# Attention, two MLPs: the fourth unit's attention by float16 halves and DMA transposes instead of transposes on TensorE

## The chip, the cores and the metric

The kernel runs on one core of one Trainium2 chip. The metric is the device time of one execution in microseconds (us). Before the change it is 997.64 us, the median of 3 runs (997.09 to 998.67).

## The reference

Causal attention with a decay (batch 4, 8 heads, 576 positions, head size 64) is followed by two MLPs on the 2304 x 512 result, with 2048 inner features each.

```python
scores = scale * np.matmul(q, k.transpose(0, 1, 3, 2))
cum = np.cumsum(np.log(np.clip(f, 0.0001, 1.0)), axis=-1)
scores = np.where(causal, -1e9, scores + cum[:, :, :, None] - cum[:, :, None, :])
attn = np.exp(scores - np.max(scores, axis=-1, keepdims=True))
attn = attn / (np.sum(attn, axis=-1, keepdims=True) + 1e-09)
x = (attn @ v) laid out as (B*S, H*D)
x = (s * np.maximum(x @ w_in, 0.0) ** 2 + b) @ w_out        # first MLP
h = x @ w_in2
out = np.maximum(0.01 * h, h) @ w_out2                       # second MLP
```

## The kernel before

**Units.** The attention and the first MLP are cut into units. Units 0 to 3 are the first 256 positions of the four batches, units 4 to 7 the last 320 positions, whose queries see up to 576 keys; unit 8 collects the last 64 positions of the four batches for the MLP. Units 0 and 1 go through the first MLP together (the loop with `u == 1`, 16 steps, `joint_step`), while the attention of unit 2 is computed beside it. Then each unit from 2 on has 16 steps of `first_mlp`, and the attention of the unit behind it is spread over those steps. The steps are counted by `n` = 16(u - 2) + i. Unit 3, the fourth, has its attention in steps 0 to 8, beside the MLP of unit 2; units 4 to 7 have theirs from step 10 on.

**One step.** `first_mlp` issues 12 matmuls into `ps_h` (`mlp1_h`, L941), then Relu, Square and a copy to float32r on ScalarE (L970 to L972) and a subtraction on VectorE (L974) that leaves the low half of g; then the 12 matmuls of an earlier step from g into `ps_o` (`mlp1_back`, `mlp1_o`, L991). From step 2 on the g used is that of two steps before. The bank of `ps_h` alternates between two, so the matmuls of step n wait until L974 of step n - 2 has read its bank. Below, H is the first group of 12, O the second.

**The attention of a pair of heads.** The heads go in pairs; p = 8 to 11 are the pairs of unit 3, 12 to 27 those of units 4 to 7. The dictionary `plan`, filled ahead by `at_step`, says what each step does; `attend`, `attend_early`, `attend_mid` and `attend_end` do it. In all units the scores are formed on TensorE (`mm_score`, L297, with the mask, L307; below, S) in one PSUM buffer `ps_s`, the maxima are taken by VectorE (`score_max`, L335), which asks SyncE for later `cumk` and `qk_p` loads (L231, L205) as it goes, and ScalarE takes the exponentials (`score_exp`, L357).

- Unit 3 (pair p scored in step 2(p - 8)): in the same step VectorE builds diagonal matrices of the reciprocal sums (`diags`, `pair_diag`, L377 to L381). In the next step TensorE multiplies the exponentials with them, which transposes and scales them (`turn_pair`, `turn`, L779), and ScalarE copies the result (L398). In the step after that TensorE multiplies with v in float32 (`pair_av`, `first_av`, L787), and `first_x` splits the result (L801, L802). v comes as it is wanted, in two loads for the whole unit (`load_v_in(3)`, L579), issued in step 14 of the joint loop.
- Units 4 to 7 (a pair in four steps): p is scaled and cut in float16 halves (`p_scale`, L403, L404; `p_high`, L421, on ScalarE; `p_low`, L426, on VectorE), and each head's halves are transposed by a DMA from SyncE (L434). The second head's `p_high`, `p_low` and transpose are issued in the next step (`carry`). Three steps after the scores `av_mm` multiplies (L484); `av_copy` (L510, ScalarE), `av_add` (L514, VectorE) and `av_end` with `split_x1` (L546, L547) finish. v takes the same road, once a pair: `load_v` (L217) into one buffer `v_raw` that all pairs share; `v_part(p, 0)`, which is `scale_v` (a maximum over v_raw, L244, three small operations, L248 to L252, on VectorE, and the high half on GpSimd, L257); `v_part(p, 1)`, which is `halve_v` (L263 on VectorE, two DMA transposes, L268) and right behind it `load_v(p + 1)`.

In units 4 to 7 the load of v for a pair is issued three steps ahead of the `v_part(.., 0)` that reads it.

**What sets the order.** All of this stands under `in_order()`: each engine, SyncE with its DMA queue included, does its instructions in exactly the order in which the code issues them. An instruction that waits holds back all behind it on its engine.

Of the kernel before, what the change touches and what calls it, by code (L numbers as in the profile page):

```python
# [8 lines left out]
F32 = mybir.dt.float32  # L9
# [8 lines left out]
P = 128  # L18
# [31 lines left out]
def attention_moe_moe_kernel(  # L50
# [748 lines left out]
    def first_x(u, pr, raw):  # L799
        x = xs[u]  # L800
        nc.scalar.copy(x[:, 0, pr], raw)  # L801
        nc.vector.tensor_tensor(out=x[:, 1, pr], in0=raw, in1=x[:, 0, pr].bitcast(F32), op=ALU.subtract)  # L802
# [14 lines left out]
    plan = {}  # L817

    def at_step(n):
        return plan.setdefault(n, {k: [] for k in ("v", "early", "s", "av", "x", "turn", "diag", "first", "load")})  # L820

    t_of = {}
    for i, (jb, *_) in enumerate(tiles):
# [1 line left out]
    nxt = 0  # L825
    for p in range(H, NP):
        ids = t_of[p]
        at_step(nxt)["s"] = ids[:2]
        if len(ids) == 2:
            at_step(nxt)["diag"] = at_step(nxt + 1)["turn"] = at_step(nxt + 2)["first"] = ids  # L830
            nxt += 2
            if len(t_of[p + 1]) > 2:
                at_step(nxt)["load"].append(p + 1)
                at_step(nxt + 1)["v"].append((p + 1, 0))
                nxt += 2
                at_step(nxt)["early"].append((p + 1, 1))
        else:
            for k in range(3):
                at_step(nxt + k)["s"] = ids[2 * k : 2 * k + 2]
                at_step(nxt + 3 + k)["av"] += ids[2 * k : 2 * k + 2]  # L840
            at_step(nxt + 6)["x"].append(ids[-1])
            if p + 1 < NP:
                at_step(nxt + 3)["early"].append((p + 1, 0))
                at_step(nxt + 4)["early"].append((p + 1, 1))
            nxt += 4
    assert max(plan) < 5 * NF

    def attend(n):
        e = at_step(n)
        first = e["s"] and len(t_of[jobs[tiles[e["s"][0]][0]][2] // 2]) == 2  # L850
        tail = e["s"] and jobs[tiles[e["s"][0]][0]][3]
        if ended:
            mlp1_end(*ended.pop())
        if e["first"]:
            k = e["first"][-1]
            first_x(3, jobs[tiles[k][0]][1] // 2, pair_av(3, k))
        if e["s"] and not tail:
            mm_score(e["s"][0])
        for i in carry:
            p_high(i)  # L860
            p_low(i)
        carry.clear()
        if tail:
            return
        for i in e["s"]:
            score_max(i)
        for i in e["s"]:
            score_exp(i)
        for p, part in e["early"]:
            v_part(p, part)  # L870
        if not first:
            for i in e["s"]:
                p_scale(i)
            for i in e["s"][:1]:
                p_high(i)
                p_low(i)
            carry.extend(e["s"][1:])

    def attend_early(n):
        diags(at_step(n)["diag"])  # L880
        for i in at_step(n)["s"]:
            if jobs[tiles[i][0]][3]:
                st_score(i)

    def attend_mid(n):
        e = at_step(n)
        turn_pair(e["turn"])
        for part in (av_mm, av_copy, av_add):
            for i in e["av"]:
                part(i)  # L890
        for i in e["s"]:
            if jobs[tiles[i][0]][3]:
                p_scale(i)
                p_high(i)
                p_low(i)
# [13 lines left out]
            load_v(p + 1)  # L909

    def attend_end(n):
        e = at_step(n)
        for p in e["load"]:
            load_v(p)
        for p, part in e["v"]:
            v_part(p, part)
        for i in e["x"]:
            av_end(i)

    hn = [0]  # L920
# [78 lines left out]
    def mlp1_end(u, po):  # L999
# [14 lines left out]
        for d in (2, 1, 0, 3) if u < 2 else range(ND):  # L1014
            x1 = x1d[d * P : (d + 1) * P, :]
            if u < 2:
                o = p_tile(F32) if d in (0, 3) else ap.tile([P, S], F32, tag="tt", name="x1o", bufs=4)[:, : 2 * UN]
                if d % 2 == 0:
                    nc.scalar.mul(o, po[d], sb[:, 0:1])
                else:  # L1020
                    nc.vector.tensor_scalar(o, po[d], sb[:, 0:1], None, ALU.mult)
                last = nc.sync.dma_start(
                    out=x1.rearrange("p (b s) -> p b s", b=B)[:, :2, :UN], in_=o.rearrange("p (b s) -> p b s", b=2)
                )
                continue
# [127 lines left out]
    def joint_step(i):  # L1153
# [19 lines left out]
        turn_pair(t)  # L1173
        if pending:
            mlp1_back(1)
        if i == NF - 2:
            load_v_in(3)
        pending.append((1, i, g))
        high(w1, c_of, i)

# [9 lines left out]
    for u in range(1, NU):  # L1190
# [12 lines left out]
        for i in range(NF):  # L1203
# [10 lines left out]
            if u < NU - 2:  # L1214
                n = (u - 2) * NF + i
                with in_order():
                    if n == 0:
                        rest.pop()()
                        for k in range(ND):
                            first_x(2, k, x_held[k])  # L1220
                    attend(n)
                    if n == 1:
                        attend_mid(n)
                        first_mlp(u, i)
                    else:
                        first_mlp(u, i, lambda: attend_early(n), lambda: attend_mid(n))
                    attend_end(n)
                continue
            with in_order():
# [98 lines left out]
```

## Time and profile before

| | |
|---|---|
| median of 3 runs | 997.64 us (997.09 to 998.67) |
| the profiled execution | 999.24 us |
| its span, first to last instruction | 997.4 us |
| PE busy | 976.8 us (98%) |
| DVE busy | 524.5 us (53%) |
| ACT busy | 506.8 us (51%) |
| GpSimd (POOL) busy | 28.3 us (3%) |

PE is TensorE's matmuls, PEld its weight loads, DVE VectorE, ACT ScalarE, SPq the DMAs that SyncE issues. "Idle before" and "<-" name how long an engine was idle ahead of an instruction and what ended that. The shares are means over the span; the stretch that the change touches lies between 130 and 192 us. A float32 matmul shows as two instructions.

### The profile page before, as it was taken

The numbers are of one execution on the slowest core, as the hardware profiler recorded it, in microseconds if no ns is written. First come the engines' busy times: TensorE is split into PE (matmuls) and PEld (weight loads), VectorE is DVE, ScalarE is ACT, GpSimd is POOL, SyncE is SP. The second block draws the span as 40 slices with busy tenths as digits, with TensorE's granted clock in tenths as the row PEclk, the third lists the DMA queues.
The fourth block names the chain that finished last, engine by engine and source line by source line (L and its number), as shares of the span: only waits on it lengthen the run. The fifth ranks groups of instructions, "written<-read, shape, count | busy, mean of one in ns | idle before, by whom it ended". The sixth has DMA issues, their size and how long they took to land.

```text
span 997.4 us, 17061 instructions
## 1 busy us (share of the span) xinstructions
PE 976.8 (98%) x6464; PEld 833.2 (84%) x6464; DVE 524.5 (53%) x1307; ACT 506.8 (51%) x1196; POOL 28.3 (3%) x100
## 2 busy tenths in 40 slices
PE   6899999999999999999999999999999999999998
PEld 5677779898888888888999998888888888888897
DVE  7797864477777777777312689783113111211121
ACT  6777766576776767767544665552122221212222
POOL 1000000000000000000000000000000000000000
PEclk9999999999999999999999999999999999999999
DMA  9744314299999998897200992003000100100010
GB/s 327 244 148 149 85 64 119 70 202 194 180 184 189 192 186 184 183 189 153 54 22 1 332 373 97 1 1 127 1 1 22 43 0 1 43 1 1 1 43 22
DMA packets 157105, 110.31 MB, mean 111 GB/s; under 512 B 110624, under 2 KB 135200, under 8 KB 157024
## 3 DMA queue, kind: packets, MB, share of 16 engines
q1 hardware_dynamic: 157024, 109.23, 43.3%
q8 instruction: 51, 0.84, 0.3%
q14 instruction: 30, 0.25, 0.1%
HBM read 74.00 MB, written 10.04 MB: 84 GB/s over the span
## 4 chain that ended last, share of the span: by engine, by line
PE 52%; ACT 0%; DVE 0%; issue 0%
PE ps_o L1091 20%; PE ps_h L1075 20%; PE ps_o L991 6%; PE ps_h L941 6%; PE ps_v L484 0%; DVE o L1103 0%; ACT tt L357 0%; ACT p_hl L421 0%; DVE g L974 0%; ACT g L972 0%; ACT ps_h L971 0%; ACT ps_h L970 0%
## 5 line engine op out<-in xcount | busy, mean ns | idle before, releaser
L941 PE MATMUL ps_h<-x_all,w 128*128 128x256 f32 (+1 forms) x1536 | 230.3, 299 | 1.7 <-ACT r_all L956 0.7
L991 PE MATMUL ps_o<-g,w 128*128 128x256 f32 (+2 forms) x1536 | 231.2, 300 | 0.0
L1091 PE MATMUL ps_o<-w,g 128*128 128x512 f32 x864 | 215.0, 395 | 0.0
L941 PEld LDWEIGHTS ps_h<-x_all,w 128*128 128x128 f32 x1536 | 202.1, 189 | 13.9 <-DVE g L974 3.9
L1075 PE MATMUL ps_h<-x,w 128*128 128x512 f32 (+1 forms) x960 | 213.5, 370 | 0.0
L991 PEld LDWEIGHTS ps_o<-g,w 128*128 128x128 f32 x1536 | 203.1, 189 | 10.7
L1075 PEld LDWEIGHTS ps_h<-x,w 128*128 128x128 f32 x960 | 169.1, 188 | 34.4
L1091 PEld LDWEIGHTS ps_o<-w,g 128*128 128x128 f32 x864 | 161.0, 188 | 37.5
L1083 DVE TENSOR_TENSOR g<-ps_h,g 128x512 fp32r<-128x512 f32 (+1 forms) x80 | 50.9, 637 | 248.8 <-ACT g L1082 248.5
L1081 ACT ACTIVATE ps_h<-ps_h 128x512 f32<-128x512 f32 (+1 forms) x80 | 43.1, 539 | 263.2 <-PE ps_h L1075 263.2
L357 ACT ACTIVATE tt<-tt,sm 128x256 f32<-128x256 f32 (+3 forms) x112 | 68.9, 616 | 76.2 <-DVE sm L335 76.2
L974 DVE TENSOR_TENSOR g<-ps_h,g 128x256 fp32r<-128x256 f32 x112 | 47.2, 421 | 86.7 <-ACT g L972 86.7
L970 ACT ACTIVATE ps_h<-ps_h 128x256 f32<-128x256 f32 x112 | 40.9, 365 | 51.9 <-PE ps_h L941 51.9
L335 DVE CUSTOM_DVE_ANT_0 tt<-ps_s,cumk 128x256 f32<-128x256 f32 (+3 forms) x112 | 54.1, 520 | 2.1 <-PE ps_s L307 0.7
L426 DVE SCALAR_TENSOR_TENSOR p_hl<-tt,sm,p_hl 128x512 f16<-128x512 f32 (+1 forms) x64 | 44.8, 700 | 15.6 <-ACT p_hl L421 14.4
L1082 ACT CAST g<-ps_h 128x512 fp32r<-128x512 f32 (+1 forms) x80 | 43.6, 544 | 6.5 <-PE ps_o L1091 4.1
L124 DVE SCALAR_TENSOR_TENSOR wt<-w_raw,wt 128x512 int32<-128x512 int32 x64 | 44.4, 694 | 2.2
L421 ACT ACTIVATE p_hl<-tt,sm 128x512 f16<-128x512 f32 (+1 forms) x64 | 42.6, 665 | 4.3 <-ACT tt L357 3.0
L972 ACT CAST g<-ps_h 128x256 fp32r<-128x256 f32 x112 | 41.8, 373 | 4.3
L971 ACT ACTIVATE ps_h<-ps_h 128x256 f32<-128x256 f32 x112 | 41.2, 368 | 3.6
L484 PE MATMUL ps_v<-p_t,v_st 128*128 128x128 f16 (+1 forms) x768 | 42.7, 209 | 0.0
L119 ACT ACTIVATE wt<-w_raw 128x512 f32<-128x512 f32 x64 | 41.0, 674 | 0.8 <-DMA w_raw<-in_moe_w_out 0.6
(123 smaller groups left out, 780.7 us busy)
## 6 DMA issues: line engine op xcount, KB each, us to landing
w_raw<-in_moe_w_in SPq DMA_DIRECT2D x32, 512.0 KB, 7.9
w_raw<-in_moe_w_out SPq DMA_DIRECT2D x32, 512.0 KB, 9.1
cumk<-cumd SPq DMA_DIRECT2D x32, 256.0 KB, 4.1
qk_p<-in_qk SPq DMA_DIRECT2D x16, 480.0 KB, 4.5
cumk<-cumd SPq DMA_DIRECT2D x32, 144.0 KB, 3.4
v_raw<-in_v SPq DMA_DIRECT2D x16, 288.0 KB, 3.3
out<-o SPq DMA_DIRECT2D x18, 256.0 KB, 2.1
x2r<-x1d SPq DMA_DIRECT2D x4, 1024.0 KB, 5.9
```

The source lines that it names most:

```text
L124: nc.vector.scalar_tensor_tensor(x, top, -0x80000000, x, ALU.bitwise_and, ALU.bitwise_or)
L335: nc.vector.tensor_tensor_reduce(tt[:, at + k0 : at + k0 + kw], ps[:, c, :kw] if half else ps[:, h % 2, at : at + w], cumk[jb][:, k0 : k0 ...
L357: nc.scalar.activation(e, e, AF.Exp, bias=sm[:, r : r + 1], scale=-1.0, accum_out=sm[:, 2 + r : 3 + r])
L426: nc.vector.scalar_tensor_tensor(v[:, 1, :w], e, inv, v[:, 0, :w], ALU.mult, ALU.subtract)
L941: nc.tensor.matmul(ps, wi[:, a, d * P : (d + 1) * P], x_all[:, :, c, d] if joint[0] else x[:, c, d], start=(d == 0 and n == 0), stop=(d == ...
L974: nc.vector.tensor_tensor(out=g[:, 1, :UN], in0=ps, in1=g[:, 0, :UN].bitcast(F32), op=ALU.subtract)
L991: nc.tensor.matmul(po[d], wo[:, a, d * P : (d + 1) * P], g[:, c], start=(first and n == 0), stop=(last and n == 2),)
L1075: nc.tensor.matmul(ps[:, :n], wi[:, a, d * P : (d + 1) * P], x[:, e, d, :n], start=(d == 0 and k == 0), stop=(d == ND - 1 and k == 2),)
L1081: nc.scalar.activation(raw, raw, AF.Lrelu)
L1082: nc.scalar.copy(g[:, 0, :n], raw)
L1083: nc.vector.tensor_tensor(out=g[:, 1, :n], in0=raw, in1=g[:, 0, :n].bitcast(F32), op=ALU.subtract)
L1091: nc.tensor.matmul(po[m], g[:, a, m * P : (m + 1) * P], wo[:, e, :], start=(i == 0 and k == 0), stop=(i == NF - 1 and k == 2),)
```

## The change

Unit 3's attention is computed as that of units 4 to 7, in a plan of two steps a pair.

- Pair p (8 to 11) is scored in step 2(p - 8) as before. `p_scale`, `p_high`, `p_low` and the first head's DMA transpose follow in that step, the second head's in the next; `av_mm` with copy and add comes three steps after the scores, `av_end` four steps after. The diagonals, the turn on PE, the copies of its result, the float32 product and `first_x` of unit 3 are gone.
- `v_part(p + 1, 0)` is issued in the odd step behind pair p's scores, `v_part(p + 1, 1)` in the next even step. The first pair's v is loaded in step 13 of the joint loop, scaled in step 15, and `v_part(8, 1)` is issued in step 0. For pair 12 `v_part` moves from steps 9 and 10 to steps 7 and 8.
- The joint MLP's end writes two of its four outputs through the buffers `p_t0` and `p_hl_t` instead of `p_hl`.
- The separate order of step 1, where the turn stood ahead of the step's matmuls, is gone.

```diff
         ids = t_of[p]
-        at_step(nxt)["s"] = ids[:2]
         if len(ids) == 2:
-            at_step(nxt)["diag"] = at_step(nxt + 1)["turn"] = at_step(nxt + 2)["first"] = ids
-            nxt += 2
-            if len(t_of[p + 1]) > 2:
-                at_step(nxt)["load"].append(p + 1)
-                at_step(nxt + 1)["v"].append((p + 1, 0))
-                nxt += 2
-                at_step(nxt)["early"].append((p + 1, 1))
+            at_step(nxt)["s"] = at_step(nxt + 3)["av"] = ids
+            at_step(nxt + 4)["x"].append(ids[-1])
+            at_step(nxt + 1)["early"].append((p + 1, 0))
+            at_step(nxt + 2)["early"].append((p + 1, 1))
+            nxt += 2 if len(t_of[p + 1]) == 2 else 4
...
     def attend(n):
         e = at_step(n)
-        first = e["s"] and len(t_of[jobs[tiles[e["s"][0]][0]][2] // 2]) == 2
...
-        if e["first"]:
-            k = e["first"][-1]
-            first_x(3, jobs[tiles[k][0]][1] // 2, pair_av(3, k))
...
         for p, part in e["early"]:
             v_part(p, part)
-        if not first:
-            for i in e["s"]:
-                p_scale(i)
-            for i in e["s"][:1]:
-                p_high(i)
-                p_low(i)
-            carry.extend(e["s"][1:])
+        for i in e["s"]:
+            p_scale(i)
+        for i in e["s"][:1]:
+            p_high(i)
+            p_low(i)
+        carry.extend(e["s"][1:])

     def attend_early(n):
-        diags(at_step(n)["diag"])
...
     def attend_mid(n):
         e = at_step(n)
-        turn_pair(e["turn"])
...
             if u < 2:
-                o = p_tile(F32) if d in (0, 3) else ap.tile([P, S], F32, tag="tt", name="x1o", bufs=4)[:, : 2 * UN]
+                if d in (0, 3):
+                    o = ap.tile([P, 5 * P], F32, tag=("p_t0", "p_hl_t")[d % 2], name="x1o", bufs=1)[:, : 2 * UN]
+                else:
+                    o = ap.tile([P, S], F32, tag="tt", name="x1o", bufs=4)[:, : 2 * UN]
...
-        if i == NF - 2:
-            load_v_in(3)
+        if i == NF - 3:
+            load_v(H)
+        if i == NF - 1:
+            v_part(H, 0)
...
                     if n == 0:
+                        at_step(n)["early"].append((H, 1))
                         rest.pop()()
...
                     attend(n)
-                    if n == 1:
-                        attend_mid(n)
-                        first_mlp(u, i)
-                    else:
-                        first_mlp(u, i, lambda: attend_early(n), lambda: attend_mid(n))
+                    first_mlp(u, i, lambda: attend_early(n), lambda: attend_mid(n))
                     attend_end(n)
```

## Rows read from the trace of the kernel before

**Rows 1.** The page, part 1: busy time, share of span, instructions.

```profile
PE 976.8 (98%) x6464; PEld 833.2 (84%) x6464; DVE 524.5 (53%) x1307; ACT 506.8 (51%) x1196; POOL 28.3 (3%) x100
```

**Rows 2.** Windows, from S of step 4 to S of step 6: us, busy by engine, clock, DMA share, GB/s.

```profile
167.93:177.01 9.08, 9.08 (x82) 8.46 (x80) 3.48 (x14) 5.22 (x17) 0.00 (x0) 1.00 0.39 100
```

**Rows 3.** Timeline, PE from H of step 5: start, length, what, idle before.

```profile
171.93 1.59 PE L941 MATMUL ps_h<-x_all,w 128*128 128x256 f32 x12
...
173.35 1.50 PE L779 MATMUL ps_t<-diag,tt 128*128 128x128 f32 x12
...
174.61 1.67 PE L991 MATMUL ps_o<-g,w 128*128 128x256 f32 x12
...
176.21 0.87 PE L787 MATMUL av<-p_t,v_in 128*64 128x256 f32 x8
...
177.01 0.92 PE L297 MATMUL ps_s<-qk_p 64*128 64x256 f32 x8
```

**Rows 4.** Timeline, PE in a step of unit 4's attention.

```profile
210.38 0.84 PE L484 MATMUL ps_v<-p_t,v_st 128*128 128x128 f16 x12
211.03 1.67 PE L991 MATMUL ps_o<-g,w 128*128 128x256 f32 x12
212.63 0.92 PE L297 MATMUL ps_s<-qk_p 64*128 64x384 f32 x4
```

**Rows 5.** Timeline: step 0 around the maxima, a load of step 6, S of step 10.

```profile
149.84 0.92 PE L297 MATMUL ps_s<-qk_p 64*128 64x256 f32 x8
...
151.13 0.42 DVE L335 CUSTOM_DVE_ANT_0 tt<-ps_s,cumk 128x256 f32<-128x256 f32 x1
...
152.24 0.08 DVE L335 DVE_READ_ACCUMULATOR2_ANT sm<- 128x1 f32 x1
...
152.78 0.38 SPq L205 DMA_DIRECT2D qk_p<-in_qk  x1
...
180.80 0.54 SPq L205 DMA_DIRECT2D qk_p<-in_qk  x1
...
191.92 1.13 PE L297 MATMUL ps_s<-qk_p 64*128 64x512 f32 x4
```

**Rows 6.** SyncE's DMA queue: v's transposes, the load behind them; all transposes of p (min/median/max ns).

```profile
195.57 2.65 SPq L268 DMA_TRANSPOSE v_st<-v_hl  x2
198.33 0.53 SPq L217 DMA_DIRECT2D v_raw<-in_v  x1
...
L434 SPq DMA_TRANSPOSE p_t<-p_hl x64: 1209/1237/2207, 199.0 to 475.4; - x64
```

**Rows 7.** From issue to landing: line L217, 288 KB; loads of 128 KB, steps 0 to 7.

```profile
DMA to landing us min/median/max: 3.1/3.3/4.1
...
cumk<-cumd SPq DMA_DIRECT2D x5, 128.0 KB, 3.4
```

**Rows 8.** Groups by form, DVE: busy us, mean ns, idle before.

```profile
L718 DVE TENSOR_REDUCE sm<-ps_s 128x1 f32<-128x256 f32 x4 | 1.7, 416 | 0.0
...
L252 DVE RECIPROCAL vs<-vs 128x1 f32<-128x1 f32 x16 | 2.6, 164 | 0.6
...
L974 DVE TENSOR_TENSOR g<-ps_h,g 128x256 fp32r<-128x256 f32 x72 | 30.2, 420 | 24.9 <-ACT g L972 24.9
...
L514 DVE TENSOR_TENSOR x_raw<-ps_v,x_raw 64x256 f32<-64x256 f32 x30 | 12.7, 422 | 5.4 <-ACT x_raw L510 5.2
...
L244 DVE TENSOR_REDUCE vs<-v_raw 128x1 f32<-128x576 f32 x16 | 11.9, 745 | 0.0
...
L426 DVE SCALAR_TENSOR_TENSOR p_hl<-tt,sm,p_hl 128x384 f16<-128x384 f32 x31 | 20.0, 647 | 5.6 <-ACT p_hl L421 5.5
```

**Rows 9.** Opening: PE behind a wait (timeline), and its clock after (windows, PE alone).

```profile
34.99 1.18 PE L679 MATMUL ps_s<-qk_p 64*128 64x128 f32 x8 [1.73 <-DMA qk_p<-in_qk]
...
36.00:37.00 1.00, 1.00 (x8) 0.50 0.60 149
...
39.00:40.00 1.00, 1.00 (x10) 1.00 0.74 157
```

More of the change, by code (lines that the diff above doesn't have):

```diff
@@ L819, in at_step @@
     def at_step(n):
-        return plan.setdefault(n, {k: [] for k in ("v", "early", "s", "av", "x", "turn", "diag", "first", "load")})
+        return plan.setdefault(n, {k: [] for k in ("early", "s", "av", "x")})
     t_of = {}
@@ L911, in attend_end @@
     def attend_end(n):
[L912 to L917, printed above, removed]
+        for i in at_step(n)["x"]:
             av_end(i)
```

## The prediction, made before the changed kernel ran

> **What bounds the kernel now.** I read the page's busy times first: TensorE (PE) is busy for 976.8 of 997.4 us, VectorE (DVE) and ScalarE (ACT) for about half [rows 1]. As the shares are means over stages, I then read the stretch that the change touches, unit 3's attention in steps 0 to 9. From one S to the next but one, two steps later, PE is busy for all of 9.08 us, DVE for 3.48, ACT for 5.22, at a granted clock of 1.00 [rows 2]. No wait of PE is listed there: PE's instructions in a row set the pace, and the other engines have 4 to 5 us of slack per pair of heads. From the first score of step 0 at 149.84 to that of step 10 at 191.92 it takes 42.08 us [rows 5]. Behind step 10 the order of the work is nearly as before, so the change is worth what it does to these 42.08 us.
>
> **Off PE.** Start to start, the turn takes 173.35 to 174.61 = 1.26 us and the float32 product 176.21 to 177.01 = 0.80 us a pair [rows 3]. The float16 product of 12 matmuls of 128 columns that takes their place lasts 0.65 us (210.38 to 211.03) [rows 4]: it has the same count here, as unit 3's heads have two and one blocks of keys in two halves, for two heads. Net 1.41 us a pair, 5.6 us for four. The sums on PE alone say 5.6 us faster.
>
> **Onto DVE.** Gone a pair are the diagonals and one subtraction of the split; added are four small operations of `p_scale` (0.16 each [rows 8]), four `p_low`, `scale_v`, `halve_v`, two `av_add` (0.42 each) and a split. `p_low` on 256 and on 128 columns is not in the trace; the row of 384 columns, 0.65, bounds it from above, and the 256-wide subtraction L974, 0.42, is about its lower end, so I take 0.53 and 0.41 (an estimate), and 0.5 each for `halve_v` and the split. With starts some 0.03 us apart: maxima 1.2 [rows 5], halve 0.5, scale 0.75, four p_low 1.9, two L974 0.9, `scale_v` 1.05, adds 0.86, split 0.5, together 7.65 us a pair. PE would need 9.08 - 1.41 = 7.67. So DVE goes from 3.5 of 9.1 us to the whole of PE's new pace, and in its fixed order it also waits some 0.8 us a pair for exponentials. The slack that hid its waits is gone.
>
> **Onto SyncE, and the wait that matters.** The change adds four DMA transposes and one load of v a pair. `halve_v` of pair p issues two transposes of v and behind them `load_v(p + 1)`; the very next step issues `scale_v(p + 1)`, whose first operation on DVE reads that load. In units 4 to 7 three steps lie between; here one. What is queued on DVE behind this wait: L974 of the odd step (which frees the bank for H two steps on), `av_add`, and the next pair's maxima, which lead to the next `halve_v`, the next transposes and the next load. So it is a loop that goes round once a pair, and I sum it. Let M be the start of a pair's maxima (151.13 in step 0).
> - SyncE first issues two `cumk` loads and one `qk` load, which is out at 153.16, so M + 2.03 [rows 5]. The maxima take to 152.32, M + 1.2, and `halve_v` is done by M + 1.75, under that.
> - Two transposes of v, then the load: from 195.57 to 198.33, 2.76 us [rows 6]. The load goes out at M + 4.8. The transposes here are smaller than the 640 columns of that row. The 64 transposes of p there have 768 or 1024 columns and still all lie near 1.24 us (1.21 at the least) [rows 6], so I take the price as fixed. The ends: 1.21 each, and, if they were as cheap as a plain load, 0.44 each (the `qk` loads took 0.38 and 0.54 [rows 5]).
> - Landing: 3.1 to 4.1 us for v at 288 KB, 3.4 for loads of 128 KB [rows 7], which is the size here; I take 3.3. It lands at M + 8.1.
> - `scale_v`: a maximum over 256 columns 0.42 and three operations of 0.16 [rows 8], with gaps 1.05; L974, 0.45. Done at M + 9.55.
> - two `av_add`, 0.86 [rows 8], then the next M: M + 10.4. Into step 2 there is no `av_add` yet: M + 9.55.
>
> Each round thus takes 10.4 us where PE needs 7.7 and took 9.08 before. M is 151.13, then 160.7, 171.1 and 181.5 in step 6. In the last round SyncE is 1.0 later, as step 6 loads more for the larger unit (the `qk` load ends at 181.34, 4.33 behind S [rows 3, 5], against 3.32 in step 0): the load of pair 12 goes out at M + 5.8, lands at M + 9.1 (288 KB); `scale_v` over 576 columns takes 0.75 + 0.6, L974 0.45: M + 10.95 = 192.45. H of step 9 waits for that. Behind it stand H 1.42 (171.93 to 173.35), the float16 product 0.65 and O 1.60 (211.03 to 212.63) [rows 3, 4]: the score of step 10 starts at 196.1 instead of 191.92. **4.2 us later.**
>
> **PE's clock.** By this sum PE idles about 1.0 us ahead of H of step 5, 2.0 ahead of step 7 and 3.5 ahead of step 9. In the opening PE came back at 34.99 after a wait of 1.73, and its granted clock was then 0.50, which is 1.2 GHz, in 36 to 37 and back at 1.00, 2.4 GHz, by 39 [rows 9]; it had been busy before, with gaps. Such a dip of about 2.8 us costs 1.4 us where PE is on the path, and here it is only behind step 9. I take half, 0.7 (ends 0 and 1.4). The earlier gaps would dip into idle time.
>
> **At no cost.** v's first load and scaling lie in steps 13 and 15 of the joint loop, where DVE waits for ACT; if not, a microsecond. The outputs of the joint end go out through other buffers, with the same work. ACT has some 6.8 us of work in 10.4, SyncE about 7 (four transposes of 1.3, four loads of 0.45).
>
> **A page beside the row.** The transpose of v takes SyncE 1.3 us each, a plain load 0.38 to 0.54 [rows 5, 6]. The Trainium skill, "Advanced Engine Details and Errata", section "X-Bar Transpose (TRN2)", says that on this chip transposing DMAs are as fast as regular ones. By the row the loop is 10.4 us a round; by that rule it would be rival 2 below.
>
> **The sum.** 4.2 + 0.7 = 4.9 us. The profiled execution took 999.24 us (span 997.4 and 1.84 around it), so 1004.1 there; it lies 1.60 above the median, so I predict **1002.5 us**.
>
> **The rivals.**
> 1. PE's sum holds whole: 997.6 - 5.6 = 992.0. For it: PE is the bound everywhere else, and H has two banks, so the first late round costs PE nothing (H of step 3 comes as late as the loop's 160.7). Against it: DVE's 7.65 leaves nothing for waits, and the lateness of each round adds up. 7%.
> 2. The load lands in time or goes out early, as with transposes of 0.44: out at M + 3.0, landed at M + 6.3, round 8.7; DVE's own work and waits, 8.4 to 8.5, are then the floor. M in step 6 is 151.13 + 8.5 + 17.4 = 177.0, L974 of step 7 done at 186.2, the score of step 10 at 189.85: 2.1 us faster, and up to 3.9 with no wait for the load at all. Time about 994.8, and this is the one on the other side, faster; it decides where a round is under some 9.3 us, that is if load and transposes together are 1.1 us quicker than summed. For it: the small v transposes are not in the trace. Against it: the even price over sizes. 14%.
> 3. Slower still: landing at 4.1 each time, as transposes of p and v share the queue, adds 0.8 a round, 3.2 in all, and a full dip of the clock 0.7 more: 1006.4. For it: in units 4 to 7 the slowest landing is 4.1. Against it: the DMA share here is 0.39 [rows 2]. 9%.
>
> **How the numbers follow.** The forecast has 70%; its own range goes from +2.6 (landing 3.1, transposes at 1.21, no dip) to +7 (landing 3.9, full dip): 1000.2 to 1004.9. For 8 in 10 the range must take in most of rival 2 and the near half of rival 3: 994.5 to 1006. About 0.2%, 2 us, is what a measurement of this kernel can tell from no change. Slower by more than that (over 999.6): nearly all of the forecast, 0.64, and rival 3, together 0.73. Within: 0.06 of the forecast and 0.04 of rival 2, 0.10. Faster: rival 1 and the rest of rival 2, 0.17.
>
> **What would show it.** Right: in the changed trace the maximum over v_raw (L244) stands idle for a DMA, about 1 us or more, in steps 1, 3, 5 and 7; the starts of the maxima lie 9.5 to 10.5 us apart; PE waits ahead of H (L941) in steps 5, 7 and 9, released by DVE's L974; two transposes of v take 2.5 us of SyncE's queue. Wrong: L244 starts without a wait, maxima 7.7 to 8.7 apart; or PE without idle time between steps 0 and 10. If DVE idles for exponentials more than for the load, the bound is DVE's and ACT's chain, and the loop only its neighbour.

## The result, and the profile after

The kernel after takes 1004.74 us, the median of 4 runs (1004.08 to 1005.98); the kernel before took 998.15 us in 4 runs beside it. The ratio is 1.0064, with a 95% interval of 1.0048 to 1.0081: slower by about 6.5 us. The profiled execution took 1005.98 us (span 1004.2), against 999.24 us (span 997.4) before. The executions of one kernel spread over 1 to 6 us, and step 0 begins between 148.6 and 152.5 us in the profiles. So each kernel below is also judged by the length from the first score of step 0 to that of step 10 in its profile. Such a length stands for one execution: experiments 4 and 11 are the same kernel and differ in it by 0.9 us. Line numbers have moved: H is now L926, O L976, the subtraction on VectorE (DVE) behind H L959.

The page's part 1 of the kernel after (busy us, share of the span, instructions; it answers to [rows 1]):

```profile
PE 975.6 (97%) x6432; PEld 832.8 (83%) x6432; DVE 537.1 (53%) x1355; ACT 511.3 (51%) x1212; POOL 31.1 (3%) x108
```

TensorE (PE) is busy 1.2 us less, DVE 12.6 more, and the execution is 6.7 us longer. A share over 1000 us can't show where. The waits of PE and DVE from 145 to 205 us can (engine, line waited for: us in total, times, longest). In the kernel before PE has none in this stretch. The kernel after has these:

```profile
DVE vs L244 <- DMA v_raw<-in_v: 12.1, 4, 4.3
...
PE ps_h L926 <- DVE g L959: 6.5, 3, 3.2
...
PE ps_v L484 <- DMA p_t<-p_hl: 1.4, 1, 1.4
...
PE ps_h L926 <- ACT x1o L1007: 0.5, 1, 0.5
```

DVE stands 12.1 us for the load of v, in four places, and PE 6.5 us for DVE's subtraction, 6.3 of them in the two waits behind the late loads. Two short waits of PE are new besides: for the transposed p, once, and for a copy of the joint MLP's output out of `ps_o`, once.

The timeline of the kernel after, PE and DVE (start, length, what, idle before), at the scores, the first maxima of each pair, the maxima over v_raw and two late H:

```profile
149.79 0.92 PE L297 MATMUL ps_s<-qk_p 64*128 64x256 f32 x8
...
151.08 0.43 DVE L335 CUSTOM_DVE_ANT_0 tt<-ps_s,cumk 128x256 f32<-128x256 f32 x1
...
158.19 0.42 DVE L244 TENSOR_REDUCE vs<-v_raw 128x1 f32<-128x256 f32 x1 [0.58 <-DMA v_raw<-in_v]
...
159.42 0.42 DVE L335 CUSTOM_DVE_ANT_0 tt<-ps_s,cumk 128x256 f32<-128x256 f32 x1
...
169.02 0.42 DVE L244 TENSOR_REDUCE vs<-v_raw 128x1 f32<-128x256 f32 x1 [4.33 <-DMA v_raw<-in_v]
...
171.13 0.42 DVE L335 CUSTOM_DVE_ANT_0 tt<-ps_s,cumk 128x256 f32<-128x256 f32 x1
...
180.60 0.42 DVE L244 TENSOR_REDUCE vs<-v_raw 128x1 f32<-128x256 f32 x1 [3.78 <-DMA v_raw<-in_v]
...
181.97 1.76 PE L926 MATMUL ps_h<-x_all,w 128*128 128x256 f32 x12 [3.15 <-DVE g L959]
...
182.71 0.42 DVE L335 CUSTOM_DVE_ANT_0 tt<-ps_s,cumk 128x256 f32<-128x256 f32 x1
...
191.83 0.75 DVE L244 TENSOR_REDUCE vs<-v_raw 128x1 f32<-128x576 f32 x1 [3.44 <-DMA v_raw<-in_v]
...
193.54 2.81 PE L926 MATMUL ps_h<-x_all,w 128*128 128x256 f32 x12 [3.15 <-DVE g L959]
...
198.85 1.13 PE L297 MATMUL ps_s<-qk_p 64*128 64x512 f32 x4
```

From step 0 to step 10 it is now 198.85 - 149.79 = 49.06 us, where it was 42.08 [rows 5]: 6.98 longer, which is about the whole result. The maxima start at 151.08, 159.42, 171.13 and 182.71: rounds of 8.34, 11.71 and 11.58 us. Each pair waits for its load of v, and the last two H shown for the DVE work behind that.

### The profile page after: what moved, and what is told of

Same layout as the page of the kernel before. It is cut to its first block, busy times and chain, and to the rows that moved or that the text cites. A ratio compares the mean times of both kernels' runs of the same rounds, so it can differ in the third digit from the quotient of the medians.

```text
span 1004.2 us, 17130 instructions
## 1 busy us (share of the span) xinstructions
PE 975.6 (97%) x6432; PEld 832.8 (83%) x6432; DVE 537.1 (53%) x1355; ACT 511.3 (51%) x1212; POOL 31.1 (3%) x108
## 4 chain that ended last, share of the span: by engine, by line
PE 52%; ACT 0%; DVE 0%; issue 0%
PE ps_o L1079 20%; PE ps_h L1063 20%; PE ps_o L976 6%; PE ps_h L926 6%; PE ps_v L484 0%; DVE o L1091 0%; ACT tt L357 0%; ACT p_hl L421 0%; DVE g L959 0%; ACT g L957 0%; ACT ps_h L956 0%; ACT ps_h L955 0%
## 5 line engine op out<-in xcount | busy, mean ns | idle before, releaser
L926 PE MATMUL ps_h<-x_all,w 128*128 128x256 f32 (+1 forms) x1536 | 231.8, 300 | 8.6 <-DVE g L959 6.5
L976 PE MATMUL ps_o<-g,w 128*128 128x256 f32 (+2 forms) x1536 | 232.4, 301 | 0.0
L926 PEld LDWEIGHTS ps_h<-x_all,w 128*128 128x128 f32 x1536 | 203.2, 190 | 21.7 <-DVE g L959 10.7
L976 PEld LDWEIGHTS ps_o<-g,w 128*128 128x128 f32 x1536 | 204.2, 190 | 10.7
L959 DVE TENSOR_TENSOR g<-ps_h,g 128x256 fp32r<-128x256 f32 x112 | 47.1, 421 | 78.2 <-ACT g L957 78.1
L426 DVE SCALAR_TENSOR_TENSOR p_hl<-tt,sm,p_hl 128x512 f16<-128x512 f32 (+2 forms) x80 | 50.9, 645 | 15.2 <-ACT p_hl L421 13.6
L421 ACT ACTIVATE p_hl<-tt,sm 128x512 f16<-128x512 f32 (+2 forms) x80 | 48.9, 621 | 4.0 <-ACT tt L357 3.3
L484 PE MATMUL ps_v<-p_t,v_st 128*128 128x128 f16 (+1 forms) x816 | 47.4, 212 | 1.4 <-DMA p_t<-p_hl 1.4
L484 PEld LDWEIGHTS <-v_st 128*128 128x128 f16 x816 | 39.1, 99 | 3.9 <-issue 1.5
```

The costliest lines, as they stand in the source:

```text
L421: nc.scalar.mul(v[:, 0, :w], e, inv)
L426: nc.vector.scalar_tensor_tensor(v[:, 1, :w], e, inv, v[:, 0, :w], ALU.mult, ALU.subtract)
L484: nc.tensor.matmul(av[:, at + e * m : at + (e + 1) * m], v_st[j + e][:, k].rearrange("p l d -> p (l d)"), pt[:, to + l * nk + k, e * m : ( ...
L926: nc.tensor.matmul(ps, wi[:, a, d * P : (d + 1) * P], x_all[:, :, c, d] if joint[0] else x[:, c, d], start=(d == 0 and n == 0), stop=(d == ...
L959: nc.vector.tensor_tensor(out=g[:, 1, :UN], in0=ps, in1=g[:, 0, :UN].bitcast(F32), op=ALU.subtract)
L976: nc.tensor.matmul(po[d], wo[:, a, d * P : (d + 1) * P], g[:, c], start=(first and n == 0), stop=(last and n == 2),)
```

## The experiments

Each edit is made on the kernel after, unless it says otherwise. Theory A is the prediction's: the loop through `halve_v`, its transposes, the load behind them and `scale_v` sets the pace. Rival B: DVE's own work is the floor (7.65 us a pair and its waits). Where A holds, a second question stands: is a round the sum of SyncE's issue times, as the prediction counted it, or is it the traffic on the DMA engines that decides when the load lands? The table gives medians, ratios to the kernel before on the same chip, the length from step 0's score to step 10's, and the three rounds of maxima (pairs 8 to 9, 9 to 10, 10 to 11).

| | median us | ratio [95%] | length | rounds |
|---|---|---|---|---|
| before | 998.15 | | 42.08 | 9.01, 9.08, 9.08 |
| after | 1004.74 | 1.0064 [1.0048, 1.0081] | 49.06 | 8.34, 11.71, 11.58 |
| 1 load ahead of the transposes | 1004.09 | 1.0057 [1.0042, 1.0072] | 47.13 | 8.08, 10.66, 10.61 |
| 2 two halves of v_raw | 1001.73 | 1.0025 [1.0007, 1.0043] | 44.16 | 8.08, 8.48, 8.19 |
| 3 pair 12 two steps later | 1002.87 | 1.0045 [1.003, 1.006] | 46.10 | 8.71, 12.04, 11.31 |
| 4 both, 2 and 3 | 996.96 | 0.9979 [0.9964, 0.9994] | 39.74 | 8.08, 9.03, 7.96 |
| 5 outputs held to steps 1 and 3 | 1009.15 | 1.0104 [1.0083, 1.0124] | 50.17 | 8.32, 11.36, 11.60 |
| 6 qk load behind v | 1001.23 | 1.0016 [1.0002, 1.003] | 45.47 | 8.06, 11.49, 9.46 |
| 7 = 4 and 5 | 998.30 | 0.9994 [0.9985, 1.0003] | 40.36 | 8.08, 7.55, 7.97 |
| 8 = 7 and 6 | 999.10 | 0.9998 [0.9986, 1.0009] | 41.68 | 8.08, 7.56, 7.96 |
| 9 outputs from GpSimd's queue | 1004.66 | 1.0050 [1.0032, 1.0067] | 49.76 | 8.37, 11.07, 11.45 |
| 10 = 4 and 9 | 997.38 | 0.9979 [0.9965, 0.9993] | 42.97 | 8.07, 13.01, 7.97 |
| 11 = 4 again | 998.07 | 0.9986 [0.9975, 0.9997] | 40.62 | 8.08, 8.59, 7.97 |
| 12 three outputs at step 9 | 1004.11 | 1.0046 [1.0027, 1.0065] | 45.59 | 8.35, 9.81, 11.52 |

**1. The load ahead of its transposes.** `halve_v` has read `v_raw` by then, so in unit 3 the next load can go out first:

```diff
 # halve_v
+        if units[heads[j][0]][2] == UN:
+            load_v(j // 2 + 1)
         for r in range(2):
 # v_part
-        if part:
+        if part and units[u][2] > UN:
             load_v(p + 1)
```

> The changed kernel, with the load of v for the next pair issued on SyncE ahead of the two transposes of v instead of behind them, in unit 3 alone. Theory (loop through the load): the load goes out 2.5 us sooner in each round (the two transposes took 2.46 to 2.59 us), so the rounds fall from 11.7 and 11.6 us to about 9.2, the last leg (maxima of step 6 to L244's end in step 7) by 2.5, the waits of L244 for the load shrink from 0.6, 4.3, 3.8 and 3.4 us to under 2; the score of step 10 about 9 us sooner than in the changed kernel: about 996. Rival (DVE is simply full with the added work, 7.65 us a pair and waits for exponentials): rounds 8.4 to 8.5 and no wait for the load left. Rival (SyncE's queue is full, whatever its order): no change, about 1004.

The load of pair 12 as an example, in the timeline of DVE (it was issued at 184.51), and in the answer for line L217 (`load_v`), its time from issue to landing in step 6:

```profile
190.81 0.75 DVE L244 TENSOR_REDUCE vs<-v_raw 128x1 f32<-128x576 f32 x1 [3.75 <-DMA v_raw<-in_v]
```

```profile
DMA to landing us min/median/max: 6.3/6.3/6.3
```

The load goes out 2.2 to 2.7 us sooner in its round and lands 3.8, 3.8, 6.0 and 6.3 us after issue, where the kernel after has 2.3, 2.3, 4.8 and 3.5. So it is there only 1.0 to 1.2 us sooner in the first three rounds, and 0.3 later in the last. The rounds shrink by 0.3 to 1.1 us instead of 2.5, so the sum of issue times alone is refuted as the price of a round. With two transposes right behind it the load takes 1.2 to 2.8 us longer to land. That they share the DMA engines would fit this, but no run here tests it by itself. The time, 1004.09, is also what the third theory on record gives (SyncE's queue is full, whatever its order); experiment 2 decides against that.

**2. Two halves of v_raw.** A pair of unit 3 needs 256 of the buffer's columns, so two fit, and each load can go out a whole round earlier:

```diff
 # load_v
-            nc.gpsimd.memset(kept["v"][:, kend:], 0.0)
-        v_raw[2 * p] = kept["v"]
+            nc.gpsimd.memset(kept["v"][:, 2 * UN :], 0.0)
+        v_raw[2 * p] = kept["v"][:, p % 2 * UN :] if un == UN else kept["v"]
 # v_part
-        if part:
+        if part and units[u][2] > UN:
             load_v(p + 1)
+        if part and units[u][2] == UN and p != t12 - 2:      # t12 = 12
+            load_v(min(p + 2, t12))
 # joint loop, step 13
             load_v(H)
+            load_v(H + 1)
```

> The changed kernel, with v of two pairs of unit 3 side by side in the one buffer v_raw (256 of its columns each), so that a pair's v is loaded two pairs ahead; pair 12, which needs the whole buffer, is loaded and scaled as in the changed kernel. Theory (loop through the load): no wait of L244 in steps 1, 3 and 5, rounds down from 11.7 and 11.6 to 8.5 or less; the wait in step 7 stays at 3 to 4 us; score of step 10 about 7 us sooner than in the changed kernel, level with the kernel before: about 998. Rival (DVE full): the same rounds of 8.4 to 8.5, but DVE busy without a gap. Rival (SyncE full): rounds stay over 10.

One wait is left of the four, that of the large pair 12, whose load needs the whole buffer (waits of DVE, 145 to 205 us):

```profile
DVE vs L244 <- DMA v_raw<-in_v: 3.6, 1, 3.6
```

The rounds are 8.08, 8.48 and 8.19 with DVE's work unchanged. That speaks for A and against B as the price: 3 us of each late round were the load. It speaks against a full queue too, with which they would stay over 10. How near B's own floor lies is seen under experiment 4. The length falls by 4.9 us, less than the 7 expected; the 2.1 that remain over before stand with the one wait left, which experiment 4 takes away.

**3. Pair 12 two steps later.** Only the last round is taken out of the loop: the v of the first large pair is scaled and halved in steps 9 and 10, as before.

```diff
 # plan
-            at_step(nxt + 1)["early"].append((p + 1, 0))
-            at_step(nxt + 2)["early"].append((p + 1, 1))
+            late = 0 if len(t_of[p + 1]) == 2 else 2
+            at_step(nxt + 1 + late)["early"].append((p + 1, 0))
+            at_step(nxt + 2 + late)["early"].append((p + 1, 1))
```

> The changed kernel, with the scaling of pair 12's v in steps 9 and 10 as in the kernel before, instead of steps 7 and 8; its load stays in step 6. Theory (loop through the load): the first three rounds stay at 8.3, 11.7 and 11.6 us, the wait of L244 in step 7 and PE's wait ahead of H of step 9 (3.15 us) with its dip of the clock go: about 5 us sooner, 1000. Rival (the lateness of the first rounds is what counts and the last leg is hidden): no change, about 1004.

No wait for the load stands in the last leg, and the length is 3.0 us shorter, less than expected: the three waits of the other rounds are still there (9.1 us on DVE). PE stands for the transposed p in step 3 as in the kernel after (1.29 us), and now in step 9 too (0.98 and 0.21 us).

**4. Both.**

> The two edits of e2 and e3 together: v of unit 3 two pairs ahead in the halves of v_raw, pair 12's v scaled in steps 9 and 10. Theory (loop through the load): no wait for a load of v is left; what remains is the larger of PE's own sum (5.6 us under the kernel before) and DVE's chain of 8.4 us a pair: 992 to 994.5, faster than the kernel before. Rival (DVE full, with ACT's exponentials in its chain): rounds 8.4 or more, PE still waits for L959: 995 or more. Rival (SyncE full): above 998.

PE's waits in the stretch, all of them:

```profile
PE ps_v L484 <- DMA p_t<-p_hl: 1.7, 1, 1.7
PE ps_h L931 <- ACT x1o L1012: 0.5, 1, 0.5
PE ps_h L931 <- DVE g L964: 0.3, 1, 0.3
```

and the first maximum of the third pair, in step 4:

```profile
170.78 0.42 DVE L335 CUSTOM_DVE_ANT_0 tt<-ps_s,cumk 128x256 f32<-128x256 f32 x1 [1.03 <-PE ps_s L307]
```

No maximum over v_raw waits any more, and here a pair's maxima wait for PE's scores, where in the kernel after PE's H waited for DVE. The window from the maxima of step 4 to those of step 6 decides about rival B (us, length, busy time and instructions of PE, PEld, DVE, ACT and POOL, granted clock, busy share of the DMA engines, GB/s), in the kernel after and here:

```profile
171.13:182.71 11.58, 8.22 (x76) 7.51 (x75) 6.44 (x26) 6.41 (x21) 0.68 (x2) 1.00 0.84 134
```

```profile
170.78:178.74 7.96, 7.96 (x76) 7.62 (x76) 6.44 (x26) 6.41 (x21) 0.67 (x2) 1.00 0.78 188
```

DVE's work is the same 6.44 us, and the round is 3.6 shorter: the load was the price in the kernel after. B stands right behind it, though. With the loads early DVE's waits in this round are for ACT alone (0.49, 0.62 and 0.17 us), and with them its work fills the 7.96 us but for 0.24, just over the 7.67 of PE's sum. The length is 39.74 us: 9.3 less than the kernel after and 2.3 less than before. At 996.96 us (10 runs, 995.36 to 999.81) it is faster than both kernels, if by little: a ratio of 0.9979 [0.9964, 0.9994] to before; made again (experiment 11) it gave 0.9986 [0.9975, 0.9997]. The 992 to 994.5 us expected were not reached; by its time alone rival B's 995 or more fits.

> e4 once more, beside e10 on one chip: 39.7 us from score to score, 0.2 to 0.3% under the kernel before.

Of the 5.6 us that PE saves, 2.3 (experiment 11: 1.5) show. PE's waits above are 2.5 us of the rest, 1.7 of them for the transposed p in step 3; the other 0.8 stay open. Nothing is saved from the score of step 6 to that of step 10 (14.97 us, before 14.91). A second loop of the same kind begins there: the transposes of v read `v_hl`, which is one buffer too, and GpSimd's high half of pair 11 waits until those of pair 10 have landed, and `halve_v` waits for it (POOL is GpSimd):

```profile
181.37 0.48 POOL L257 TENSOR_SCALAR v_hl<-v_raw,vs 128x256 f16<-128x256 f32 x1 [3.93 <-DMA v_st<-v_hl]
```

```profile
181.89 0.49 DVE L263 SCALAR_TENSOR_TENSOR v_hl<-v_raw,vs,v_hl 128x256 f16<-128x256 f32 x1 [1.95 <-POOL v_hl L257]
```

In experiments 7, 8 and 11 DVE waits 3.56, 1.84 and 2.79 us there; in the kernel after it does not. What this costs in time was not tested: no run gives `v_hl` a second half.

**5, 9 and 12. What makes the second round long.** The second round (11.71) is 1.3 us over the predicted 10.4, although its load landed in 2.3 us. SyncE's queue in the kernel after tells when the load went out (start, length, what):

```profile
153.20 2.59 SPq L268 DMA_TRANSPOSE v_st<-v_hl  x2
155.88 0.53 SPq L217 DMA_DIRECT2D v_raw<-in_v  x1
156.51 1.21 SPq L434 DMA_TRANSPOSE p_t<-p_hl  x1
157.78 2.27 SPq L1010 DMA_DIRECT2D x1d<-x1o  x4
160.14 2.38 SPq L434 DMA_TRANSPOSE p_t<-p_hl  x1
162.61 1.01 SPq L231 DMA_DIRECT2D cumk<-cumd  x2
...
164.19 2.47 SPq L268 DMA_TRANSPOSE v_st<-v_hl  x2
166.71 0.57 SPq L217 DMA_DIRECT2D v_raw<-in_v  x1
```

The queue has no gap from step 0 to step 3. The four writes of the joint MLP's outputs (L1010) take 2.27 us and the one transpose of p behind them 2.38, twice as long as the one ahead (1.21). Step 2's `cumk` loads are therefore issued at 162.61, 3.2 us behind its maxima, and the load of v 7.29 behind them instead of 4.8. Three edits tell whether it is the writes' turn in the queue or their traffic. Experiment 5 holds them back, two to step 1 and two to step 3:

```diff
 # mlp1_end, units 0 and 1
-                last = nc.sync.dma_start(out=x1..., in_=o...)
+                held.append((x1, o))
 # attend_end(n)
+        for x1, o in [held.pop(0) for _ in held[:2]] if n in (1, 3) else ():
+            nc.sync.dma_start(out=x1..., in_=o...)
```

> The changed kernel, with the four writes of the joint MLP's end taken from between step 0's two transposes of p on SyncE's queue: two are issued at the end of step 1, two at the end of step 3. In the changed kernel the second round took 11.7 us because the cumk and qk loads of step 2 and all behind them stood 2.5 us late on SyncE. Theory (the loop, with SyncE's queue in it): cumk in step 2 is issued 0.7 us behind the maxima instead of 3.2; two writes still stand ahead, so the second round falls by 1 to 2.5 us to 9.2 to 10.7, the others stay; from the score of step 0 to that of step 10 46.5 to 48 us instead of 49.1. Rival (the transposes of p are slow for themselves, 2.4 us then, and the writes are beside the point): second round unchanged.

Not as expected: 50.17 us, and a second round of 11.36. Two writes alone still take 2.07 us of the queue. The load of v goes out 5.88 us behind its maxima instead of 7.29, but lands 3.3 us after issue instead of 2.3, and most of the gain is gone. Its time also holds a later opening (step 0 begins 2.7 us later than in the kernel after), which the edit does not touch; two runs don't tell more.

Experiment 9 takes the writes out of SyncE's queue but not off the DMA engines. It also changes how they travel: from GpSimd they go through another queue (`software_dynamic`) and land 5.1 us after issue, where they took 4.2:

```diff
 # mlp1_end, units 0 and 1
-                last = nc.sync.dma_start(
+                last = nc.gpsimd.dma_start(
```

> The changed kernel, with the four writes of the joint MLP's end issued from GpSimd's queue instead of SyncE's, at the same place. In the changed kernel SyncE was issuing without a gap from step 0 to step 2, and the second round took 11.7 us; moving the writes behind the second transposes of p (e5) left it at 11.4. Theory (SyncE's own issue time is what is short in the first round, 10.3 us of it in a round of 8.3): cumk of step 2 is issued 0.7 us behind the maxima, the second round falls to 9.3 to 10, the others stay; from the score of step 0 to that of step 10 47 to 48 instead of 49.1 us. Rival (the writes' traffic on the DMA engines is what is short): round 2 stays over 11.

SyncE's queue there, from the transposes of p on:

```profile
155.43 3.96 SPq L434 DMA_TRANSPOSE p_t<-p_hl  x2
159.48 2.37 SPq L231 DMA_DIRECT2D cumk<-cumd  x2
```

The writes have gone from this queue, and its other DMAs have become longer: two transposes of p take 3.96 us (2.55 in step 2 of the same run), two `cumk` loads 2.37 (0.88 in step 0). The second round is 11.07, where 9.3 to 10 were expected if their turn in the queue was the price: that theory is refuted as the main price, and the rival on record, the writes' traffic, holds. With the writes in flight the queue issues slowly; how traffic does that, no run shows. The window of the second round in the kernel after, from maxima to maxima (columns as under experiment 4):

```profile
159.42:171.13 11.71, 10.33 (x96) 9.86 (x95) 6.04 (x26) 6.01 (x20) 1.09 (x3) 1.00 0.80 195
```

The DMA engines are busy for 0.80 of the second round and 0.84 of the third (under experiment 4), where the kernel before had 0.39 [rows 2]. The share alone sets neither price: in the second round it is 0.80, and the load of v still lands in 2.3 us.

Experiment 12 keeps one write in step 0 and moves the other three (with a buffer of their own for one) behind the loop, to step 9:

```diff
 # mlp1_end, units 0 and 1: d == 1 uses r_all's buffer
-                last = nc.sync.dma_start(out=x1..., in_=o...)
+                if d != 2:
+                    held.append((x1, o))
+                    continue
+                nc.sync.dma_start(out=x1..., in_=o...)
 # attend_end(n)
+        while n == 9 and held:
+            x1, o = held.pop(0)
+            nc.sync.dma_start(out=x1..., in_=o...)
```

> The changed kernel, with three of the four writes of the joint MLP's end held until the end of step 9 (one of them from the buffer r_all, idle until then); one write stays in step 0. e9 took the writes off SyncE and left the second round at 11.1 us against 11.7, with SyncE's own issues of step 1 and 2 drawn out (two transposes of p 4.0 us, two cumk loads 2.4). Theory (the traffic of the four writes on the DMA engines holds up what is issued behind it): with 0.25 instead of 1 MB these issues are back at 2.5 and 0.9 us, cumk of step 2 is issued 0.7 us behind the maxima, the second round falls to 9.3 to 9.8 us; later rounds stay; 46.5 to 47.5 us from score to score instead of 49.1. Rival (the second round is long for another reason): it stays over 11.

SyncE's queue behind the write (the second pair's maxima start at 160.43, the third's at 170.24):

```profile
159.43 1.29 SPq L434 DMA_TRANSPOSE p_t<-p_hl  x1
161.09 1.41 SPq L231 DMA_DIRECT2D cumk<-cumd  x2
```

The transpose behind the write is back at 1.29 us, `cumk` goes out 0.66 behind the maxima, and the second round is 9.81, at the edge of what was expected and 1.9 less than in the kernel after. The window of this round (columns as above):

```profile
160.43:170.24 9.81, 9.81 (x93) 9.47 (x92) 6.04 (x27) 6.01 (x20) 1.08 (x3) 1.00 0.83 153
```

The share of the DMA engines is no lower than in the kernel after; what is less is the data, 153 GB/s over 9.81 us for 195 over 11.71, or about 0.8 MB, the size of the three writes. PE's wait for the transposed p in step 3 is gone too. The third round (11.52) stays.

**6. What makes the third round long.** Ahead of the transposes SyncE issues the next but one pair's `qk_p`, 480 KB for unit 4's pairs, from step 4 on. Here that load goes behind the load of v:

```diff
 # score_max
-        if last_of_pair(jb):
+        if last_of_pair(jb) and u != 3:
             load_pair(j // 2 + 2)
 # v_part, behind load_v
+        if part and u == 3:
+            load_pair(p + 2)
```

> The changed kernel, with the qk load of steps 0, 2, 4 and 6 issued behind the load of v instead of ahead of the transposes of v. In the changed kernel the load of v landed 2.3 us after its issue in steps 0 and 2, where a qk load of 256 KB went ahead, and 4.8 and 3.5 us after it in steps 4 and 6, where it was one of 480 KB. Theory (landing is the time that the data queued ahead takes on the DMA engines): landing about 2.3 to 3 us in all four, the load out 0.4 to 0.5 sooner, the third round from 11.6 to about 9, the last leg 1 sooner; 45 to 46.5 us from score to score instead of 49.1. Rival (the transposes set the landing, whatever load goes ahead): third round stays over 11.

Landing of L217 in step 4, and the maxima at both ends of the third round:

```profile
DMA to landing us min/median/max: 3.1/3.1/3.1
```

```profile
171.02 0.42 DVE L335 CUSTOM_DVE_ANT_0 tt<-ps_s,cumk 128x256 f32<-128x256 f32 x1
...
180.48 0.42 DVE L335 CUSTOM_DVE_ANT_0 tt<-ps_s,cumk 128x256 f32<-128x256 f32 x1
```

3.1 us in step 4, where the kernel after has

```profile
DMA to landing us min/median/max: 4.8/4.8/4.8
```

The third round falls from 11.58 to 9.46 us, the length to 45.47, as expected. The 480 KB ahead of the small load were the price: 1.7 us in its landing and 0.5 in its place in the queue (issued 4.18 us behind the maxima instead of 4.64).

**7, 8 and 10. The same moves on top of experiment 4.** They were to bring more of PE's 5.6 us.

> The edits of e4 (v two pairs ahead, pair 12 scaled in steps 9 and 10) with the writes taken out of the way as in e5. e4 took 39.7 us from score to score; left in it was a wait of TensorE of 1.7 us in step 3 for the second head's transposed p, which stood behind the writes on SyncE. Theory: that wait goes, about 38 us from score to score, 4 us under the kernel before: 993 to 996. Rival (DVE and ACT's chain is the bound then): no change against e4, 996 to 997.

> e7 with the qk loads behind the v loads as in e6. With no wait for the load of v left, the order of these loads should not matter: as e7 within 0.5 us. Rival (the DMA engines are what is short, with or without the loop): a further microsecond or more either way.

> e4 (v two pairs ahead, pair 12 scaled in steps 9 and 10) with the four writes on GpSimd's queue as in e9. Theory: TensorE's wait of 1.7 us in step 3 for the transposed p goes too; 38 us from score to score against 39.7 in e4 and 42.1 before: 994 to 996. Rival (DVE's and ACT's chain is the bound): as e4.

None did: 40.36, 41.68 and 42.97 us, against 39.74 and 40.62. By time they are no faster either; experiment 10 equals experiment 4 in its ratio though its profile is 3.2 us longer, so one profile's length can lie that far from the median. In 7 the wait of 1.7 us for the transposed p in step 3 is gone and the second round takes 7.55, below the 7.67 of PE's sum, but four such waits stand elsewhere (1.9 us together, 1.17 of them in step 7); in 8 they are 3.2 us, 2.35 in step 9. In 10 the wait in step 3 grew:

```profile
165.36 0.80 PE L484 MATMUL ps_v<-p_t,v_st 128*128 128x128 f16 x6 [3.15 <-DMA p_t<-p_hl]
```

Once the load of v is early, the transposed p is what comes last in these runs, and each write or load that is moved moves that wait. A version without it was not found; experiment 12's edit, under which that wait in step 3 was gone, was not run on top of experiment 4. The other theory on record for experiment 7, that DVE and ACT are the bound then, fits as well: in 7 and 8 the rounds are 8.08, 7.55 or 7.56, and 7.97 or 7.96, with no wait of DVE in them but for ACT. No run tells the two apart.

## Why the prediction was right, step by step

It gave 1002.5 us (994.5 to 1006), slower, at 0.73; the time is 1004.74. In the profile, 4.9 us were predicted and 6.98 measured, 2.1 more. The direction and the mechanism held; three terms were mis-sized. Of the signs named ahead, the waits for the load came (0.58, 4.33, 3.78 and 3.44 us; the first is under the 1 us named) and so did the price of the transposes. The rounds of 9.5 to 10.5 us did not: 8.34, 11.71 and 11.58 lie on both sides. The time lies in the upper part of the range, where the forecast's own part ended (+7), and partly by luck, as the first round's -1.2 offsets one of the late ones. That end was added up wrongly as well: landing 3.9 in four rounds and a full dip give 4.9 + 2.4 + 0.7 = +8.0, not +7.

- **What bounds the kernel**, PE without a gap: held, and so did the warning that the stretch decides [rows 2].
- **Off PE**, 1.41 us a pair: the float16 product takes 0.65 to 0.66 us at full clock, as predicted. Experiment 4's 7.66 us from the score of step 4 to that of step 6 (169.49 to 177.15, PE busy throughout) shows PE's sum of 7.67 to be reachable.
- **Onto DVE**: the single terms were near or below the estimates (two `p_low` 0.75 for 0.94, `halve_v` 0.48 and the split 0.49 for 0.5 each). The sum was too high: 7.65 us a pair and no slack were predicted, and DVE is busy for 6.46, 6.04 and 6.44 us of the three rounds, in the kernel after as in experiment 4. The floor of 8.4 to 8.5 us that rival 2 used was a little too high with it: with the loads early, rounds in which DVE waited for ACT alone took 7.55 to 8.08. As nothing rested on it but rival 2, it cost nothing.
- **Onto SyncE, the loop**: A's mechanism is shown by experiments 2 and 4, where the wait goes and the time with it. Two transposes of v took 2.46 to 2.59 us, as the even price of [rows 6] said. By rounds: the first took 8.34 for 9.55 predicted (-1.2, since its load landed in 2.3 us and not 3.3), the second 11.71 for 10.4 (+1.3), the third 11.58 for 10.4 (+1.2), and from M of step 6 to H of step 9 10.83 for 10.95 (-0.1).
- **PE's waits ahead of H**: 1.0, 2.0 and 3.5 us were predicted for steps 5, 7 and 9. Step 5 has none (step 6 has 0.21), steps 7 and 9 have 3.15 each. PE stood 1.9 us elsewhere before, 1.38 of them for the transposed p in step 3, which the prediction did not have; that is not on the loop's path.
- **Landing, 3.3 us**: the step that failed, in both directions: 2.3, 2.3, 4.8 and 3.5 us. Of the 4.8, 1.7 is the 480 KB `qk_p` ahead of it (experiment 6). I had counted that load as one more instruction, not as traffic. The price came from units 4 to 7 [rows 7]. The DMA engines are no quieter there (window of the kernel before, columns as under experiment 4):

```profile
208.00:300.00 92.00, 91.14 (x836) 78.92 (x834) 68.97 (x212) 64.33 (x162) 7.09 (x17) 1.00 0.94 191
```

  What differs is the place in the queue: a `qk_p` of 480 KB there goes out at 206.77, 7.35 us ahead of the load of v at 214.12 (kernel before); in step 4 of the kernel after it is 2.99 us ahead.
- **`cumk` and `qk` out at M + 2.03**: held in steps 0 and 4, failed in step 2 (M + 4.67), where the queue still issued. That is **at no cost** failing: "the same work" through other buffers is 1 MB that meets the loop's own transposes. The kernel before made these writes in step 0 as well, in 1.87 us of issues and landing 2.6 us after issue instead of 4.2, but with no transpose of v or p beside them. Experiments 9 and 12 show the writes' part.
- **PE's clock, 0.7 us**: from H of step 9 to the score of step 10 it took 5.31 us for 4.37. The reason is in these windows of the kernel after (us, length, PE's busy time and instructions, granted clock, share of the DMA engines, which can come out over 1 in a window this short, GB/s):

```profile
180.00:181.00 1.00, 0.00 (x0) 1.00 1.28 287
184.00:185.00 1.00, 1.00 (x11) 0.50 0.33 119
187.00:188.00 1.00, 1.00 (x9) 1.00 0.71 135
192.00:193.00 1.00, 0.00 (x0) 1.00 0.78 170
195.00:196.00 1.00, 1.00 (x7) 0.50 0.00 0
```

  PE stood idle in 180 to 181 and in 192 to 193, and each time its clock was then 0.50, 1.2 GHz, in a later window; in 187 to 188 it is back at 1.00, 2.4 GHz. The second dip is on the path: 5.31 - 3.67 = 1.64 us, a full one (1.4 was its estimate), where I had taken half. The first lay in idle time, as predicted.
- **A page beside the row.** The loop was 11.6 us in two of three rounds, not rival 2's 8.7. The Trainium skill ("Advanced Engine Details and Errata", section "X-Bar Transpose (TRN2)"), by which transposing DMAs are as fast as regular ones, does not agree with this queue: 1.23 to 1.30 us a transpose, 0.53 to 0.63 a load of v. From issue to landing the two do lie close in step 0 of this trace: 2.5 to 3.6 us for the transposes of v, 2.3 for the load of v, 3.7 for that of `qk_p`.
- **Rival 3**, the load landing later: the nearest in time (1006.4). Its argument against, a DMA share of 0.39 in [rows 2], was the share of the kernel before. The change itself raises it to 0.80 and 0.84, yet at 0.80 the load landed in 2.3 us: the share was the wrong thing to look at, for the rival and against it.

The terms give -1.2 + 1.3 + 1.2 - 0.1 + 0.9 = 2.1 us, which is the difference.

## What to carry to other kernels

A buffer that was loaded three steps ahead becomes a loop when the steps between fall to one: sum once round it (queue, landing, first reader, and what releases the next load), and if the sum is over the engine's own pace, give the buffer a second half before anything else; here that and the old place for the one large load turned +6.5 us into -1.4 to -2.1. Take landing times from a place in the queue with the same loads ahead, not from an average over a stretch: here a small load landed in 4.8 us instead of 2.3 behind a large one, in 3.8 with two transposes right behind it, and in 6.0 with both. Issuing it 2.5 us earlier in the same round gained 1 us (experiment 1), and issuing other transfers from another queue little (experiment 9), as the same bytes were in flight; issuing it a round earlier took its wait away (experiment 2). A saving on the bounding engine is worth only as much as the next latest arrival allows: of 5.6 us, 2.3.

## What the runs showed of the hardware that was not expected

- Traffic of another queue shows in the issuing queue: with the outputs' 1 MB in flight from GpSimd's queue two transposes took SyncE 3.96 us to issue instead of 2.55, two loads 2.37 instead of 0.88 (experiment 9).
- Why the clock falls after one wait and not after another stays open. In experiment 12 PE waits 3.10 us ahead of H of step 7 and 3.13 ahead of H of step 9. After the first the clock is 0.50, after the second it stays at 1.00 (timeline of PE, then windows of PE):

```profile
181.03 2.93 PE L933 MATMUL ps_h<-x_all,w 128*128 128x256 f32 x12 [3.10 <-DVE g L966]
...
192.59 1.70 PE L933 MATMUL ps_h<-x_all,w 128*128 128x256 f32 x12 [3.13 <-DVE g L966]
```

```profile
182.00:183.00 1.00, 1.00 (x7) 0.50 0.00 0
193.00:195.00 2.00, 2.00 (x25) 1.00 0.00 0
```

- Whether the rest of PE's 5.6 us can be had is open as well: with the load early, the transposed p comes last, and no run here moved the product that reads it a step later, or gave `v_hl` a second half.
